# A first attention block copied out in two parts, and three pieces of a fused kernel's schedule moved

## The chip, the core and the metric

One core of a Trainium2 chip. The metric is the device time of one execution in microseconds (us); the median of several runs is compared.

## What is computed

Three stages follow one another: attention over 2 x 768 tokens with 8 heads of 64, in which a query sees the 8 first keys and the 96 before it; then a feed-forward block with a mish gate; then four experts with relu, weighted by probabilities. Everything is fp32.

```python
scores = scale * np.matmul(q, k.transpose(0, 1, 3, 2)) + bias
scores = np.where(keep, scores, -1000000000.0)
a = np.exp(scores - np.max(scores, axis=-1, keepdims=True))
x = np.matmul(a / (np.sum(a, axis=-1, keepdims=True) + 1e-09), v)
...
h = x @ w_in
g = h * np.tanh(np.where(h > 20.0, h, np.log1p(np.exp(np.minimum(h, 20.0)))))
x = g @ w_out
...
p = domain_probs / (domain_probs.sum(-1, keepdims=True) + 1e-09)
for e in range(E):
    out += p[:, e:e + 1] * (np.maximum(x @ w1[e], 0.0) @ w2[e])
```

## The kernel before, in words

The 1536 tokens are three blocks of 512. An attention tile is 128 queries by two heads (a pair); a block has 16 pairs. Weights come in chunks: 16 of the feed-forward block, 32 of the experts. Each chunk is one step: a hidden product (`hidden`, L648: 12 matmuls of 128x512) into a PSUM bank, an activation, and an output product (`project`, L737: 12 matmuls). Fast matmuls take fp32 values as two halves, a high one (names ending in h, a ScalarE cast) and a low one (ending in l, a subtraction). `part` makes them of a weight chunk: ACT casts `wh` (L630), POOL subtracts `wl` in two operations (L633).

The kernel runs in this order. First the attention of block 0 and its feed-forward steps 0 to 15 (`first_block`). Its order is written out by hand as a string, `PLAN`: each letter is one stage of one pair or chunk. `F` copies a row tile of the attention's result from PSUM into `x0` (`take`, L412), four tiles in all, by ScalarE; the last copy is what the first hidden product (L778) waits for. `Q` is the last output product (L825), which ends the block: `end_ffn` copies the result to `y0h` on ACT (L754) and subtracts `y0l` on DVE (L755), in four operations each. Letters near the end of the string begin the second attention, of blocks 1 and 2: `j` splits one more pair's q and k (ACT casts qs and kh, L239 and L241; the subtractions are on POOL for the first two pairs, on DVE from the third), `z` makes the probabilities on DVE, `4` is `norm` and `parts`, `2` and `3` are scores and softmax of the first pair, `6` is the step of a round that multiplies by the values. `norm` takes the reciprocal of the sums on DVE (L192, L193) and scales the probabilities p: on ACT for the first three pairs (L198), on POOL for the others (L200). `parts` splits pairs up to two ahead, and the values v (ACT L254, POOL L255).

Then a loop over the remaining steps s. From s = 16 the expert steps of block 0 run, and each carries one round of the second attention: scores of pair r (L265, L266), softmax (`gather` of an older pair's result on DVE L329 and L332, with casts on ACT L333 and POOL L334; then L279 on DVE and exponentials on ACT, L290), transposes of pair r - 1 on PE (L205) with their cast on ACT (L302) and subtraction on DVE (L303), norm of pair r, parts, and the value product of pair r - 2 (L312), copied by ACT (L320). Three steps (`EXTRA`, s = 27, 35 and 43) carry two rounds, one before the step's own. The weight chunk two steps ahead is parted at the head of every step. PE, ACT, DVE and POOL each take their instructions in the order in which the program issues them. A transpose of pair r reads p after its scaling; POOL stands at whatever instruction is next in its order.

Of the kernel before, what the change touches and what calls it, by code (L numbers as in the profile page):

```python
# [16 lines left out]
P = 128  # L17
B, H, S, D = 2, 8, 768, 64
DM = H * D
NP = H // 2  # L20
NT = S // P
NTOK = B * S
TB = 512
# [20 lines left out]
    "SSYXXESYSEXSEDXNXESNTDCTXSENAZNEXATTSCZEDAXANSFSNEXTTDCNEZAXANTETSCZaADXNAtSFNTEXSCTXEAZSEDAVSVaXTTX"  # L44
    "CSEZAEADVVFTXTCEZAAaDVVTtTCaAZtAFttttttHecttHanltueHvgtcetatntluHvcgnlyettPuvaacHttentPyytlHguvacttH"
    "tbagetnluseyvPcgtbPtbybnPbbbbsluavHcgtnltyyeuvPcgsHnlytaPtuvgtaPyttetatcntstHlseuvcHgtstneluaHvePHcn"
    "tgtluyvcPsgtenlHuvcwgatnliseuvPcHyttjrntlegryyPuyvcsnlwH12yPguevcngl3wuvghPhwwwowowz4Qywj6"
)

AFTER = {  # L50
# [109 lines left out]
class Pair:  # L160
# [47 lines left out]
    def take(self):  # L208

        xh, xl = self.body.x[self.t]  # L210
        at = slice(None), self.pr, slice(self.col, self.col + P)
        heads = [(slice(j * 64, (j + 1) * 64), slice(j * P, (j + 1) * P)) for j in range(2)]
        for r, c in heads:
            self.nc.scalar.copy(xh[at][r, :], self.o[r, c])
        for r, c in heads:
            self.nc.vector.tensor_tensor(xl[at][r, :], self.o[r, c], xh.bitcast(F32)[at][r, :], ALU.subtract)
# [120 lines left out]
class FirstPair(NarrowPair):  # L337
# [71 lines left out]

    def take(self, engine):  # L410

        engine(self.body.x0[:, :, self.col:self.col + P], self.body.o.rearrange("p (n q) -> p n q", n=NP))  # L412


class WidePair(Pair):
# [128 lines left out]
class Body:  # L544
# [420 lines left out]
    def flush(self):  # L965
        for run in self.later:
            run()
        self.later = []
# [35 lines left out]
    def late_block(self, project):  # L1004
# [22 lines left out]
        for run in held[:2]:  # L1027
            run()
# [9 lines left out]
        for run in held[2:]:  # L1038
            run()
# [30 lines left out]
    def first_block(self, ready, now):  # L1070
# [4 lines left out]
        then = Attention(self, self.pair, 1, NB - 1)  # L1075
        n = dict.fromkeys("SXEDNTCAFHecnluvgPatwbsyrhoz", 0)
# [103 lines left out]
        def begin_next(k):  # L1180
# [5 lines left out]
            "S": scores, "X": pair("biased"), "E": pair("exps"), "D": inverse, "N": scale(nc.gpsimd), "V": scale(nc.vector), "T": pair("trans"),  # L1186
            "C": pair("copy", nc.scalar.copy), "Z": pair("copy", nc.vector.tensor_copy), "A": pair("av"),
            "F": take(nc.scalar.copy), "G": take(nc.vector.tensor_copy), "a": begin, "t": convert, "w": part,
            "Y": warm, "H": hidden, "e": self.mish_exp, "c": self.mish_cap, "n": self.mish_n, "l": self.mish_r,
            "u": self.mish_u, "v": self.mish_v, "g": self.gate_first, "P": project, "Q": last,  # L1190
# [1 line left out]
            "b": x_part, "s": split, "y": store,  # L1192
            "z": lambda k: self.probabilities(), "r": second, "h": self.mish_hi, "o": self.mish_lo,
            "1": lambda k: then.ahead(), "2": lambda k: then.scores(), "3": lambda k: then.softmax(),
            "4": lambda k: (then.norm(), then.parts()), "5": lambda k: then.trans(), "6": lambda k: then.av(),
        }
        same = dict(Z="C", G="F", V="N")
        for token in PLAN:
# [11 lines left out]
    def run(self):  # L1210
# [6 lines left out]
        last = len(steps)  # L1217
# [16 lines left out]
        def now(what, upto):  # L1234
            while ready[what] < min(upto, last):
                for _ in getattr(self, what)(ready[what]) or ():
                    pass
                ready[what] += 1
# [3 lines left out]
        if self.first:  # L1242
            att, done = self.first_block(ready, now)
            s0 = NF1
        else:
            att, done, s0 = Attention(self, self.pair, 0), 0, 0
# [4 lines left out]
        for s in range(s0, last):  # L1251
            if s == NF1 and not att:
                att = Attention(self, self.pair, 1, NB - 1)
            if s == need[1]:
                while att and att.round():
                    pass
                att = None
                self.attending.close()
                self.late = self.ctx.enter_context(tc.tile_pool(name="late", bufs=1))
            if self.wide and s < NF1:  # L1260
                while ready["narrow"] < min(s + 3, NF1):
                    now("fetch", ready["narrow"] + 1)
                    now("narrow", ready["narrow"] + 1)
            if ffn_at(s - 1) and done < s:
                self.mish_newton(s - 1)
            if s == NF1 and done < s:

                self.mish_hi(s - 1)
                self.mish_lo(s - 1)
                self.project(s - 2)  # L1270
                self.project(s - 1)
                done = s
            now("part", min(s + 3, last))
            if att:
                att.ahead()
            rest, att = (att, None) if s == need[0] - 2 else (None, att)
            extra = att and s - NF1 in EXTRA
            if extra:
                att.scores()
                att.softmax()  # L1280
            self.hidden(s)
            if extra:
                att.trans()
                att.norm()
                att.parts()
                att.av()
                att.ahead()
            if att:
                att.scores()
            if ffn_at(s):  # L1290
                self.mish_exp(s)
            else:
                self.relu_hi(s)
            if att:
                att.softmax()
            if not ffn_at(s):
                self.relu_lo(s)
            if ffn_at(s - 1) and done < s:
                self.mish_hi(s - 1)
            if ffn_at(s):  # L1300
                self.mish_cap(s)
                self.mish_n(s)
                self.mish_r(s)

                if ffn_at(s - 1):
                    self.mish_lo(s - 1)
            if not self.wide or ready["narrow"] == NF1:
                now("fetch", s + 6)
            follow = bool(s0) and s == NF1 + 1
            if follow:  # L1310
                self.project(done)
                done += 1
            if att and not extra:
                att.trans()
                att.norm()
                att.parts()
            if ffn_at(s - 1) and not ffn_at(s) and done < s:
                self.mish_lo(s - 1)
            if not follow and done <= s - (1 if s0 and att and s < need[0] - 2 else 2):
                self.project(done)  # L1320
                done += 1
            if extra:
                att.trans()
                att.norm()
                att.parts()
            if att and not att.av():
                att = None
            att = att or rest
            for task in {8: (("weights", 0, "in"), ("weights", 1, "in")), 6: (("sums", 0),), 5: (("sums", 1),),
                         3: (("part", 0, "in"), ("weights", 0, "out")), 2: (("part", 0, "sums"),),  # L1330
                         1: (("part", 1, "in"),)}.get(last - s, ()):
                getattr(self, "late_" + task[0])(*task[1:])
# [64 lines left out]
```

## Time and profile before

| what | value |
|---|---|
| median of 3 runs | 882.5 us (881.11 to 882.75) |
| the profiled execution | 882.74 us |
| its span, first to last instruction | 880.9 us |
| mean granted clock of TensorE | 0.997 of full speed |
| busy share of PE, DVE, ACT, POOL | 98%, 65%, 56%, 46% |
| HBM read, written | 97.02 MB, 28.31 MB |

The span is the time between the first and the last instruction; the profiled execution is 1.8 us longer. PE is TensorE's matmuls, PEld its weight loads, ACT ScalarE, DVE VectorE, POOL GpSimd, SP the engine that issues most transfers. In rows of a timeline the bracket is the time for which the engine sat idle before the instruction, and what ended it. Neighbouring records of one engine overlap by up to 0.1 us or so, since an operation begins while the one before it drains.

### The profile page before, as it was taken

How to read it: one execution, taken by the hardware profiler on the slowest of the kernel's cores; microseconds unless marked ns; L12 is line 12 of the kernel's file. 1: busy time of each engine (PE TensorE's matmuls, PEld its weight loads, DVE VectorE, ACT ScalarE, POOL GpSimd, SP SyncE). 2: the span in 40 equal slices, each digit the busy share in tenths (PEclk: the TensorE clock that was granted, in tenths of full speed). 3: DMA queues.
4: the chain of work that ended last, by engine and by line, in shares of the span. 5: the costliest groups of instructions: out<-in, count | busy, mean ns of one | idle time of the engine just before them, and what ended most of it. 6: DMA issues, size and time to landing. Idle time of an engine off the chain costs nothing.

```text
span 880.9 us, 11412 instructions
## 1 busy us (share of the span) xinstructions
PE 865.2 (98%) x3892; PEld 677.8 (77%) x3892; DVE 575.1 (65%) x1108; ACT 495.1 (56%) x971; POOL 407.5 (46%) x431
## 2 busy tenths in 40 slices
PE   8899998999999999999999999999999999999997
PEld 4545656888888888888888888788888888888886
DVE  6999996766777775566656667645555555555555
ACT  6667576878877777577675567533333333333330
POOL 4001333777776877555310225554455555544420
PEclk9999999999999999999999999999999999999999
DMA  8479782444444442888555640511111111111002
GB/s 316 171 247 282 263 310 96 162 171 145 168 144 145 167 168 73 307 290 289 223 194 198 241 167 1 186 54 48 48 48 48 49 57 62 49 48 48 1 1 99
DMA packets 40579, 127.47 MB, mean 145 GB/s; under 512 B 4160, under 2 KB 6976, under 8 KB 38464
## 3 DMA queue, kind: packets, MB, share of 16 engines
q1 hardware_dynamic: 39648, 125.32, 40.6%
q0 software_dynamic: 720, 1.31, 0.8%
q8 instruction: 32, 0.52, 0.2%
q14 instruction: 35, 0.29, 0.1%
q10 hardware_dynamic: 144, 0.02, 0.0%
HBM read 97.02 MB, written 28.31 MB: 142 GB/s over the span
## 4 chain that ended last, share of the span: by engine, by line
PE 80%; DVE 9%; DMA 4%; issue 2%; ACT 2%; POOL 1%; SPq 0%; DVEq 0%; ACTq 0%; POOLq 0%
PE acc_l L985 20%; PE acc L737 19%; PE h L648 18%; PE ha L934 9%; PE hx L934 7%; DMA wfirst<-w 2%; PE pt L205 2%; DVE w L612 2%; PE o L312 1%; DVE w L614 1%; DMA qk<-in_qk 1%; DVE w L610 1%; PE acc L821 1%; DVE nr L688 1%; PE s L266 1%
## 5 line engine op out<-in xcount | busy, mean ns | idle before, releaser
L633 POOL TENSOR_TENSOR wl<-w,wh 128x512 fp32r<-128x512 f32 x94 | 123.6, 1335 | 67.5 <-ACT wh L630 54.3
L838 DVE SCALAR_TENSOR_TENSOR big<-acc_l,prob,big 128x512 f32<-128x512 f32 x120 | 88.8, 746 | 78.9 <-PE acc_l L985 78.7
L917 POOL TENSOR_TENSOR zl<-wout,zh 128x512 fp32r<-128x512 f32 x32 | 40.9, 1303 | 85.2 <-ACT zh L915 85.2
L917 POOL TENSOR_TENSOR sumsl<-bias,sumsh 128x512 fp32r<-128x512 f32 x32 | 42.7, 1355 | 69.3 <-ACT sumsh L915 69.3
L947 ACT COPY raw<-ha 128x512 f32<-128x512 f32 x33 | 19.4, 586 | 79.6 <-PE ha L934 79.6
L684 DVE SCALAR_TENSOR_TENSOR nr<-e,n 128x512 f32<-128x512 f32 x48 | 34.1, 711 | 44.1 <-ACT n L679 43.8
L664 ACT ACTIVATE e<-h 128x512 f32<-128x512 f32 x48 | 28.1, 586 | 60.8 <-PE h L648 25.5
L200 POOL TENSOR_SCALAR p<-p,st 128x256 f32<-128x256 f32 (+1 forms) x58 | 41.5, 726 | 36.6 <-ACT v L254 31.9
L648 PE MATMUL h<-y0h,wh 128*128 128x512 f32 x128 | 51.0, 398 | 2.1 <-ACT y0h L754 1.9
L737 PE MATMUL acc<-wh,gh 128*128 128x512 f32 x128 | 52.4, 409 | 0.0
L648 PE MATMUL h<-y0l,wh 128*128 128x512 f32 x128 | 51.0, 398 | 0.7 <-DVE y0l L755 0.7
L648 PE MATMUL h<-y0h,wl 128*128 128x512 f32 x128 | 50.9, 398 | 0.0
L985 PE MATMUL acc_l<-zh,gh 128*128 128x512 f32 x128 | 50.7, 396 | 0.0
L985 PE MATMUL acc_l<-zh,gl 128*128 128x512 f32 x128 | 50.5, 394 | 0.0
L630 ACT CAST wh<-w 128x1024 fp32r<-128x1024 f32 x48 | 50.1, 1045 | 0.7
L985 PE MATMUL acc_l<-zl,gh 128*128 128x512 f32 x128 | 50.4, 394 | 0.0
L737 PE MATMUL acc<-wh,gl 128*128 128x512 f32 x128 | 50.2, 392 | 0.0
L985 PE MATMUL acc_l<-zh,gl_late 128*128 128x512 f32 (+1 forms) x128 | 50.0, 391 | 0.0
L985 PE MATMUL acc_l<-zh,gh_late 128*128 128x512 f32 (+1 forms) x128 | 50.0, 391 | 0.0
L737 PE MATMUL acc<-wl,gh 128*128 128x512 f32 x128 | 50.0, 390 | 0.0
L737 PE MATMUL acc<-gh,wh 128*128 128x512 f32 x128 | 49.8, 389 | 0.0
L737 PE MATMUL acc<-gh,wl 128*128 128x512 f32 x128 | 49.8, 389 | 0.0
(254 smaller groups left out, 2521.3 us busy)
## 6 DMA issues: line engine op xcount, KB each, us to landing
w<-in_wts SPq DMA_DIRECT2D x32, 512.0 KB, 4.6
raw<-in_qkv SPq DMA_DIRECT2D x32, 512.0 KB, 3.6
big<-in_wff SPq DMA_DIRECT2D x10, 1024.0 KB, 6.4
wfirst<-w SPq DMA_DIRECT2D x16, 512.0 KB, 11.0
w<-wfirst SPq DMA_DIRECT2D x16, 512.0 KB, 4.7
wkeep<-wh SPq DMA_DIRECT2D x16, 512.0 KB, 4.0
wkeep<-wl SPq DMA_DIRECT2D x16, 512.0 KB, 3.0
wh<-wkeep SPq DMA_DIRECT2D x16, 512.0 KB, 3.2
```

The source lines that it names most:

```text
L200: nc.gpsimd.tensor_scalar(p, p, r, 0.0, ALU.mult, ALU.add)
L630: (nc.vector.tensor_copy if copy == "vector" else nc.scalar.copy)(hi, w)
L633: getattr(nc, engine or "gpsimd").tensor_tensor(lo[:, c], w[:, c], hi.bitcast(F32)[:, c], ALU.subtract)
L648: nc.tensor.matmul(ps, a[:, c], r[:, kc, :], start=m == 0, stop=m == 3 * KC - 1)
L664: nc.scalar.activation(e, self.h[s], AF.Exp, scale=0.5)
L684: nc.vector.scalar_tensor_tensor(self.nr[s], e, 1.0, n, ALU.add, ALU.mult)
L737: nc.tensor.matmul(acc[:, h], a, r, start=opens and k == 0 and m == 0, stop=closes and k == len(chunks) - 1 and m == 2)
L838: nc.vector.scalar_tensor_tensor(o, acc, p, o, ALU.mult, ALU.add)
L917: nc.gpsimd.tensor_tensor(lo[:, c], w[:, c], hi.bitcast(F32)[:, c], ALU.subtract)
L934: nc.tensor.matmul(ps, a[:, c], r[:, kc, :], start=opens and n == 0, stop=n == 5, skip_group_check=True)
L947: nc.scalar.copy(t[(1, 6, 7).index(m)], ps)
L985: nc.tensor.matmul(o, a[:, c], r[:, w], start=n == 0, stop=n == 5)
```

## The change

The last of the four copies of the first attention's result is made in two operations, the first of them of one block of 128 columns. In the plan, `j` (one more pair split) goes ahead of `z`, `4` is `norm` alone, and `parts` becomes a letter of its own, `7`, behind `Q`. In the loop, `norm` goes ahead of `trans`, and in the three steps with two rounds the parting of the weight chunk goes from the head of the step to behind the second softmax.

```diff
-    "...tgtluyvcPsgtenlHuvcwgatnliseuvPcHyttjrntlegryyPuyvcsnlwH12yPguevcngl3wuvghPhwwwowowz4Qywj6"
+    "...tgtluyvcPsgtenlHuvcwgatnliseuvPcHyttjrntlegryyPuyvcsnlwH12yPguevcngl3wuvghPhwwwowowjz4Q7yw6"
...
     def take(self, engine):
 
-        engine(self.body.x0[:, :, self.col:self.col + P], self.body.o.rearrange("p (n q) -> p n q", n=NP))
+        o = self.body.o.rearrange("p (n q) -> p n q", n=NP)
+        for n in (slice(0, 1), slice(1, NP)) if self.col + P == TB else (slice(0, NP),):
+            engine(self.body.x0[:, n, self.col:self.col + P], o[:, n, :])
...
-            "4": lambda k: (then.norm(), then.parts()), "5": lambda k: then.trans(), "6": lambda k: then.av(),
+            "4": lambda k: then.norm(), "7": lambda k: then.parts(), "5": lambda k: then.trans(), "6": lambda k: then.av(),
...
-            now("part", min(s + 3, last))
             if att:
                 att.ahead()
             rest, att = (att, None) if s == need[0] - 2 else (None, att)
             extra = att and s - NF1 in EXTRA
-            if extra:
+            if not extra:
+                now("part", min(s + 3, last))
+            else:
                 att.scores()
                 att.softmax()
             self.hidden(s)
             if extra:
+                att.norm()
                 att.trans()
-                att.norm()
                 att.parts()
                 att.av()
                 att.ahead()
...
             if not ffn_at(s):
                 self.relu_lo(s)
+            if extra:
+                now("part", min(s + 3, last))
...
             if att and not extra:
+                att.norm()
                 att.trans()
-                att.norm()
                 att.parts()
...
             if extra:
+                att.norm()
                 att.trans()
-                att.norm()
                 att.parts()
```

The orders of PE and SP are the same before and after. ACT at the end of the first block, before (qs4_1 and kh4_1 are the second pair's operands, qs4_2 and kh4_2 the third's, v4_0 the first pair's values, acc0 the output product's banks):

```order
L630 CAST wh18_1186<-w18_973 128x1024
L198 ACTIVATE p4_0_1159<-p4_0_1159,st4_0_1161 128x256 x2
L239 CAST qs4_1_1201<-raw0_122 128x256
L241 CAST kh4_1_1203<-raw0_122 128x512
L239 CAST qs4_2_1208<-raw1_123 128x256
L241 CAST kh4_2_1210<-raw1_123 128x512
L254 CAST v4_0_1215<-raw0_122 128x2x2x64
L754 CAST y0h_1242<-acc0_0_683 128x512
```

And now, on the same engine at the same place:

```order
L632 CAST wh18_1187<-w18_974 128x1024
L239 CAST qs4_1_1193<-raw0_122 128x256
L241 CAST kh4_1_1195<-raw0_122 128x512
L198 ACTIVATE p4_0_1160<-p4_0_1160,st4_0_1162 128x256 x2
L756 CAST y0h_1233<-acc0_0_684 128x512
L756 CAST y0h_1233<-acc0_1_685 128x512
L756 CAST y0h_1233<-acc0_2_686 128x512
L756 CAST y0h_1233<-acc0_3_687 128x512
L239 CAST qs4_2_1243<-raw1_123 128x256
L241 CAST kh4_2_1245<-raw1_123 128x512
L254 CAST v4_0_1250<-raw0_122 128x2x2x64
```

Two casts went ahead of the scaling, three behind the four y0h copies. On DVE the third pair's subtractions went behind the four y0l subtractions in the same way.

POOL in the first step with two rounds, before (p7_0 and p7_1 are the probabilities of the step's two pairs, wl29 the low half of the weight chunk):

```order
L633 TENSOR_TENSOR wl29_2160<-w29_1948,wh29_2159 128x512 x2
L334 TENSOR_TENSOR x1l_1388<-of6_1_2170,x1h_1387 128x128
L200 TENSOR_SCALAR p7_0_2177<-p7_0_2177,st7_0_2179 128x256 x2
L255 TENSOR_TENSOR v7_0_2214<-raw0_122,v7_0_2214 128x2x128
L334 TENSOR_TENSOR x1l_1388<-of6_2_2230,x1h_1387 128x128
L200 TENSOR_SCALAR p7_1_2237<-p7_1_2237,st7_1_2239 128x256 x2
```

And now, at the same place:

```order
L334 TENSOR_TENSOR x1l_1389<-of6_1_2166,x1h_1388 128x128
L200 TENSOR_SCALAR p7_0_2173<-p7_0_2173,st7_0_2175 128x256 x2
L255 TENSOR_TENSOR v7_0_2210<-raw0_122,v7_0_2210 128x2x128
L334 TENSOR_TENSOR x1l_1389<-of6_2_2226,x1h_1388 128x128
L635 TENSOR_TENSOR wl29_2243<-w29_1949,wh29_2242 128x512 x2
L200 TENSOR_SCALAR p7_1_2233<-p7_1_2233,st7_1_2235 128x256 x2
```

The weight's two subtractions went from ahead of the first pair's scaling to right ahead of the second pair's.

ACT in the same step, now (gh27 is the step's relu, wh29 the cast that the subtractions wait for; before, it stood ahead of the first pair's x1h cast):

```order
L714 ACTIVATE gh27_2224<-h27_2180 128x512
L333 CAST x1h_1388<-of6_2_2226 128x128
L290 ACTIVATE p7_1_2233,st7_1_2235<-t7_1_2234,st7_1_2235 128x256 x2
L632 CAST wh29_2242<-w29_1949 128x1024
L302 CAST pt7_0_2270<-pt7_0_2265 128x4x128
```

The cast now stands behind the second pair's exponentials and ahead of the cast of the first pair's transposes.

## Rows read from the trace of the kernel before

**Rows 1.** Page, part 1: busy us (share of the span) xinstructions of each engine

```profile
PE 865.2 (98%) x3892; PEld 677.8 (77%) x3892; DVE 575.1 (65%) x1108; ACT 495.1 (56%) x971; POOL 407.5 (46%) x431
```

**Rows 2.** Chain of waits: start us, us, what, one product of a step

```profile
171.34 2.76 PE h L648 x12
```

**Rows 3.** PE's waits, 125 to 345 us: releaser, us in total, times, longest

```profile
PE pt L205 <- POOL p L200: 1.1, 3, 0.4
...
PE h L783 <- ACT halfh L790: 0.5, 1, 0.5
```

**Rows 4.** Timeline, 139 to 150 us: start us, us, engine line op out<-in xcount [idle <-releaser]

```profile
139.99 0.17 DVE L193 RECIPROCAL st<-st 128x2 f32<-128x2 f32 x1
...
140.25 0.91 ACT L198 ACTIVATE p<-p,st 128x256 f32<-128x256 f32 x2 [2.00 <-DVE st L193]
...
141.37 0.40 PE L825 MATMUL acc<-gl,zh 128*128 128x512 f32 x1
...
142.83 1.58 DVE L246 TENSOR_TENSOR kl<-raw,kh 128x512 fp32r<-128x512 f32 x1
...
143.01 2.03 ACT L754 CAST y0h<-acc 128x512 fp32r<-128x512 f32 x4
...
143.64 0.50 PE L648 MATMUL h<-y0h,wh 128*128 128x512 f32 x1 [1.87 <-ACT y0h L754]
...
144.34 2.47 DVE L755 TENSOR_TENSOR y0l<-acc,y0h 128x512 fp32r<-128x512 f32 x4
...
145.07 0.50 PE L648 MATMUL h<-y0l,wh 128*128 128x512 f32 x1 [0.70 <-DVE y0l L755]
...
149.05 0.28 PE L265 MATMUL s<-kh,qs 128*128 128x256 f32 x1
```

**Rows 5.** Windows: stretch, then busy us of PE, PEld, DVE, ACT, POOL; granted clock; DMA

```profile
145.50:148.90 3.40, 3.40 (x10) 2.63 (x9) 1.31 (x3) 0.00 (x0) 0.75 (x1) 0.50 0.80 295
```

**Rows 6.** Timeline at 37 us, the first block's last copy

```profile
36.44 1.22 DVE L614 SCALAR_TENSOR_TENSOR w<-big,w 128x1024 int32<-128x1024 int32 x1
37.28 0.58 ACT L412 COPY x<-o 128x512 f32<-128x512 f32 x1 [0.66 <-PE o L407]
...
37.92 8.42 PE L778 MATMUL h<-x,w 128*128 128x512 f32 x19 [0.69 <-ACT x L412]
```

**Rows 7.** Timeline, 218 to 231 us, first extra round

```profile
218.38 0.54 ACT L320 COPY p<-o 64x128 f32<-64x128 f32 x2 [0.62 <-PE o L312]
...
220.08 2.54 POOL L633 TENSOR_TENSOR wl<-w,wh 128x512 fp32r<-128x512 f32 x2 [0.54 <-ACT wh L630]
...
220.29 0.30 ACT L333 CAST x1h<-of 128x128 fp32r<-128x128 f32 x1 [0.29 <-DVE of L332]
...
226.97 0.57 ACT L302 CAST pt<-pt 128x512 fp32r<-128x512 f32 x1
...
228.71 1.51 POOL L200 TENSOR_SCALAR p<-p,st 128x256 f32<-128x256 f32 x2 [2.43 <-ACT v L254]
...
230.27 0.55 PE L205 MATMUL pt<-ident,p 128*128 128x128 f32 x3 [0.41 <-POOL p L200]
```

**Rows 8.** Timeline of PE at 167 us

```profile
167.57 0.55 PE L205 MATMUL pt<-ident,p 128*128 128x128 f32 x3 [0.26 <-POOL p L200]
```

**Rows 9.** Page, part 5: ScalarE's cast of a weight chunk, busy us, mean ns

```profile
L630 ACT CAST wh<-w 128x1024 fp32r<-128x1024 f32 x48 | 50.1, 1045 | 0.7
```

**Rows 10.** Timeline, 284 to 288 us, second extra round

```profile
284.91 0.57 ACT L302 CAST pt<-pt 128x512 fp32r<-128x512 f32 x1
...
286.65 1.51 POOL L200 TENSOR_SCALAR p<-p,st 128x256 f32<-128x256 f32 x2 [2.42 <-ACT v L254]
```

**Rows 11.** Timeline, 341 to 345 us, third extra round

```profile
341.54 0.56 ACT L302 CAST pt<-pt 128x512 fp32r<-128x512 f32 x1
...
343.27 0.93 POOL L200 TENSOR_SCALAR p<-p,st 128x256 f32<-128x256 f32 x2 [2.27 <-DVE st L193]
...
344.37 0.60 PE L205 MATMUL pt<-ident,p 128*128 128x128 f32 x4
```

More of the change, by code (lines that the diff above doesn't have):

```diff
@@ L46 @@
     "tbagetnluseyvPcgtbPtbybnPbbbbsluavHcgtnltyyeuvPcgsHnlytaPtuvgtaPyttetatcntstHlseuvcHgtstneluaHvePHcn"
-    "tgtluyvcPsgtenlHuvcwgatnliseuvPcHyttjrntlegryyPuyvcsnlwH12yPguevcngl3wuvghPhwwwowowz4Qywj6"
+    "tgtluyvcPsgtenlHuvcwgatnliseuvPcHyttjrntlegryyPuyvcsnlwH12yPguevcngl3wuvghPhwwwowowjz4Q7yw6"
 )
```

## The prediction

> **What bounds the kernel now.** I read the page first: PE is busy for 98% of the span, the other engines for 46 to 65% [rows 1]. So a change off PE is worth what it takes from, or adds to, PE's waits and PE's rate, and nothing else. The chain of waits shows the rate where nothing disturbs it: twelve 128x512 matmuls of one step's hidden product in 2.76 us, 0.23 each [rows 2]. The list of PE's waits between 125 and 345 us, the stretch that the change touches, is short [rows 3]. Two of its lines matter here: the transposes wait for POOL's scaled probabilities three times (1.1 us together), and one product of the first block waits 0.5 us for ScalarE. The two waits behind the first block's end are in the timeline: PE's last output matmul is issued at 141.37, and the next product starts at 143.64 after 1.87 us of idling for the first y0h copy, then stops 0.70 us more for the first y0l subtraction [rows 4]. And this pause costs twice: the granted clock of the following stretch is 0.50, which is 1.2 instead of 2.4 GHz, with PE busy throughout [rows 5]. From the third matmul at 145.07 to the scores at 149.05 there are ten matmuls in 3.98 us, 0.40 each; at 0.23 they would take 2.3. A fall of the clock costs 1.7 us here.
>
> **The change, part by part.** PE's and SP's own orders stay as they are; only what ACT, DVE and POOL do, and when, moves.
>
> *The last copy in two.* Before, the copy of 128x512 takes 0.58 us and the first product starts at 37.92, after 0.69 us of waiting for it [rows 6]. A cast of 128x128 on this engine takes 0.30 [rows 7], so that operand would be there some 0.3 us sooner; the other three blocks are due only after the first block's matmuls. But the same matmul also needs the first weight chunk, and DVE's last operation on that one ends at 36.44 + 1.22 = 37.66 [rows 6]. That caps the gain at about 0.2 us. At the far end of this stretch PE waits 0.5 us for a ScalarE copy that does not come from PE [rows 3], so a PE that is 0.2 ahead waits 0.2 longer there. I take 0; the ends are 0 and -0.2, and the extra operation on ACT is covered by ACT's wait for that product.
>
> *The hand-over at 140 us.* Before, five casts of the coming attention stand on ACT between the scaling (from 140.25) and the y0h copies (from 143.01), and on DVE the third pair's difference (142.83, 1.58 us) stands ahead of the y0l subtractions (144.34) [rows 4]. The change moves two of the casts into the 2.00 us in which ACT waits for DVE's reciprocal, and three behind the y0h copies; DVE's difference goes behind the y0l subtractions. The new times: the reciprocal is there at 139.99 + 0.17, the scaling ends at 140.25 + 0.91 = 141.1 (records overlap a little), the first y0h copy follows. In the trace the first product starts 0.63 after that copy's start (143.01 to 143.64), so now at 141.7, when PE has just issued its last output matmul. DVE is free and starts on y0l at 141.7; its first result reached PE 0.73 after its start before (144.34 to 145.07), so 142.45 now, and the fourth one comes 3 x 0.62 later (2.47 for four), at 144.3 [rows 4]. PE has one matmul left then: the scores start at 144.6, against 149.05. That is 4.4 us: 1.9 of idling, 0.8 of the second wait, and 1.7 because a PE that hardly stops keeps its clock. What was moved back is needed later: the third pair's operands are ready on DVE some 2 us behind 144.2 (1.58 for the larger one, as before), and are due at the scores behind the next product, another 2.76 and a few small matmuls later, near 148; the value cast's reader comes later still. I see no wait that takes the place. Bounds: -2.7 if the clock falls all the same, -4.6 if nothing waits at all.
>
> *Norm ahead of the transposes.* The reciprocal's two small DVE operations (0.17 each) [rows 4] go ahead of a subtraction that waits for ACT's cast anyway, so POOL can scale about a microsecond sooner. That removes the 0.26 us at 167.57 [rows 8]. I take -0.3 with the restart; the ends are 0 and -0.5.
>
> *The weight parts in the three extra rounds.* Here the change adds a wait. Before, ACT's cast of the weight chunk stood at the head of the round, in time in which ACT then waited for DVE anyway: the next cast comes 0.29 after it, released by DVE [rows 7]. Taking it away brings the chain of the round forward by nothing, since the chain starts with PE's output (218.38, released by PE) [rows 7]. Now the cast stands behind the second pair's exponentials, and POOL's pair of subtractions for that chunk stands between them and the second pair's scaling, for which PE's transposes already waited in rounds one and two. Round one: ACT is free behind the exponentials at 226.97; the two small operations on DVE now run inside a wait, for which I take 0.2 off; the cast takes 1.05 [rows 9]; POOL's subtractions 2.54; the scaling 0.93 to 1.51. The sum with 0.93 is 231.3, and PE went on at 230.27: +1.0 [rows 7]. Round two: 284.91 - 0.3 + 1.05 + 2.54 + 0.93 = 289.1 against 286.65 + 1.51 = 288.2: +1.0 [rows 7, 10]. Round three had no wait: 341.54 + 1.05 + 2.54 + 0.93 = 346.1 against transposes at 344.37, whose second half is due 0.1 later: +1.6 [rows 11]. Together +3.6. I take 0.93 for the scaling because POOL reaches it later, when DVE is done with its own two-input subtraction; in the third round, where no pair is left to subtract, it takes 0.93 before too [rows 11]. At 1.51 the rounds cost 0.6 more each, +5.3. The other end is nothing at all, rival one.
>
> The Trainium skill (GPSIMD Engine Reference, Specifications) says that GpSimd shares its SBUF interfaces with VectorE and contends with VectorE instructions of two SBUF inputs. The trace agrees as far as it goes (1.51 with such an instruction about, 0.93 without one); by that rule alone, with DVE beside it, the sum would take the +5.3.
>
> **Sum.** The profiled execution took 882.74: -4.4 - 0.3 + 3.6 = -1.1. The median of the runs is 882.5, 0.24 lower; on that scale the forecast is 881.4. What a measurement of this kernel can tell from no change is about 0.2%, 1.8 us. So the likeliest case is a small gain that is not clearly told from none.
>
> **Rivals.**
>
> One: the extra rounds cost nothing. The ACT chain would have to start sooner once the weight cast has left the head of the round, by the full 3.6 of cast and subtractions, or POOL would have to have slack. For it: POOL idled 2.43 us ahead of the scaling at 228.71 [rows 7]. Against: the new work is 2.54 plus 1.05, and it cannot start before the exponentials. The time: 882.5 - 4.7 = 877.8.
>
> Two, the slower one: the clock falls at the three new waits. By the sums above PE would wait 1 to 1.5 us in each round, and 0.4 more between its transposes, not far from the 1.87 and 0.70 behind which the clock fell at the hand-over [rows 4, 5]. Against it: PE is busy up to each wait and right behind it. Each fall costs the 1.7 of above. One gives 883.1, two 884.8, three 881.4 + 5.1 = 886.5; from the second on the kernel is slower than before.
>
> The Trainium skill (TensorE: Matmul & The Clock Gate, Part 1: The HAM clock gate) says that the low clock is the default and that PE's activity is what lifts it. By that rule every pause of PE is a candidate, and all three falls would give 886.5; the hand-over agrees (0.50 behind the pause), while the three short waits of now, up to 0.4 us, show no fall.
>
> Three: the hand-over gains less, because the clock falls in spite of the shorter pause, or POOL's half of the second pair is late for the scores. For it: the reciprocal's wait on DVE stays, and it lies ahead of everything else. The gain would be 2.7, the time 883.1.
>
> That the change does not do what it says I leave out: the order of every engine shows it.
>
> **How the numbers follow.** Forecast 0.55, rival one 0.17, rival two 0.18 (0.07 for one fall, 0.11 for two or three), rival three 0.10. The forecast's own range is 879.6 to 883.1: the lower end with a scaling that waits for less, the upper one with the scaling at 1.51. About 0.21 of its 0.55 lies below 880.7, where a gain would show. Faster: 0.21 + 0.17 = 0.38. Slower: 0.11 and 0.03 from the upper ends = 0.14. The same: 0.48. The range goes down to rival one, 877.8, and up to two falls, 884.8.
>
> **What would show it.** Right: the first product behind the first block starts within 0.2 us of PE's last output matmul, the granted clock stays at 1.00 there, and the scores come some 4.4 us sooner. The wait at 167.57 is gone. In each of the three extra rounds the list of PE's waits has the transposes on POOL's scaling with 1 us or more, and POOL's subtractions of the weight stand right ahead of that scaling. Wrong: a granted clock of 0.50 in one of these rounds, POOL's scaling ending no later than before relative to the round's start, a new wait of PE for y0l, or a first product that starts by 0.2 sooner at 38 us with the gain still there at 125.

## The result and the profile after

The changed kernel takes 887.13 us (median of 4 runs, 886.09 to 887.48) against 881.81 of the kernel before in the same comparison; the ratio is 1.0058 (95% interval 1.0044 to 1.0072). It is slower by 0.6%, outside the forecast's range. The profiled execution took 887.48, 4.74 more than that of before. The page's line of busy times, beside [rows 1]:

```profile
PE 867.5 (98%) x3892; PEld 679.0 (77%) x3892; DVE 590.6 (67%) x1108; ACT 495.1 (56%) x972; POOL 401.0 (45%) x431
```

PE is still the engine that counts. What the shares do not show is that its instructions now come sooner at 150 us and later at 350. The same places in both profiled executions, by PE's timeline:

| PE starts | before | after | difference |
|---|---|---|---|
| scores behind the hand-over | 149.05 | 144.60 | -4.45 |
| hidden product behind the old stall at 167.57 | 171.17 | 166.26 | -4.91 |
| first round with two pairs | 217.89 | 212.98 | -4.91 |
| its output product behind the transposes that wait | 230.58 | 227.48 | -3.10 |
| next hidden product | 233.90 | 232.38 | -1.52 |
| second such round: that output product | 288.52 | 289.44 | +0.92 |
| next hidden product | 291.82 | 294.34 | +2.52 |
| third such round: that output product | 344.72 | 349.18 | +4.46 |
| next hidden product | 348.05 | 352.50 | +4.45 |
| end of the span | 880.9 | 885.7 | +4.8 |

The hand-over and the stall behind it came out as forecast. By the table, from the start of the first round to each next hidden product, the three rounds cost 3.39, 4.04 and 1.93; that is 9.36 where 3.6 was forecast. The hand-over in the timeline after, the answer to [rows 4]:

```profile
140.00 0.91 ACT L198 ACTIVATE p<-p,st 128x256 f32<-128x256 f32 x2 [1.18 <-DVE st L193]
140.82 2.03 ACT L756 CAST y0h<-acc 128x512 fp32r<-128x512 f32 x4
...
141.42 2.48 DVE L757 TENSOR_TENSOR y0l<-acc,y0h 128x512 fp32r<-128x512 f32 x4 [1.51 <-ACT y0h L756]
141.44 0.50 PE L650 MATMUL h<-y0h,wh 128*128 128x512 f32 x1
...
144.60 0.28 PE L265 MATMUL s<-kh,qs 128*128 128x256 f32 x1
```

The copies start right behind the scaling, PE goes on without a bracket, and the scores come at 144.60, where the forecast had put them. Not all of the 4.45 belongs to the hand-over: the last output product ahead of it was issued at 141.37 before and at 141.11 after. From there to the scores it is 7.68 before and 3.49 after, so the hand-over itself gives 4.19. The windows of the same stretch show a PE that never stops and a clock of 1.00 (columns: PE, PEld, DVE, ACT, POOL busy in the window, granted clock, DMA share, GB/s):

```profile
140.00:142.00 2.00, 2.00 (x9) 1.21 (x7) 0.58 (x1) 2.00 (x5) 1.84 (x3) 1.00 0.00 0
142.00:144.00 2.00, 2.00 (x9) 1.52 (x9) 1.97 (x5) 1.98 (x5) 1.14 (x1) 1.00 0.00 0
144.00:146.00 2.00, 2.00 (x15) 1.78 (x14) 1.97 (x5) 0.71 (x2) 1.95 (x2) 1.00 0.12 14
```

The loss, in the first of the three rounds, in the timeline after (beside [rows 7]):

```profile
221.95 1.04 ACT L632 CAST wh<-w 128x1024 fp32r<-128x1024 f32 x1
...
223.06 2.71 POOL L635 TENSOR_TENSOR wl<-w,wh 128x512 fp32r<-128x512 f32 x2 [1.81 <-ACT wh L632]
224.67 1.65 DVE L246 TENSOR_TENSOR kl<-raw,kh 128x512 fp32r<-128x512 f32 x1
225.75 1.37 POOL L200 TENSOR_SCALAR p<-p,st 128x256 f32<-128x256 f32 x2
226.72 1.00 PE L205 MATMUL pt<-ident,p 128*128 128x128 f32 x4 [1.95 <-POOL p L200]
...
228.38 0.63 PE L739 MATMUL acc<-wh,gh 128*128 128x512 f32 x1
...
282.50 0.71 PE L312 MATMUL o<-pt,v 128*128 128x256 f32 x4 [0.65 <-DVE of L332]
...
288.68 1.02 PE L205 MATMUL pt<-ident,p 128*128 128x128 f32 x4 [1.98 <-POOL p L200]
...
345.37 2.53 POOL L635 TENSOR_TENSOR wl<-w,wh 128x512 fp32r<-128x512 f32 x2 [1.80 <-ACT wh L632]
347.88 0.94 POOL L200 TENSOR_SCALAR p<-p,st 128x256 f32<-128x256 f32 x2
...
348.42 1.00 PE L205 MATMUL pt<-ident,p 128*128 128x128 f32 x4 [1.37 <-POOL p L200]
```

Read it downwards: POOL idles 1.81 us for the cast, subtracts for 2.71, only then scales, and PE stands for 1.95. Then the matmuls behind it take 0.63 a record instead of 0.39. The later rows are the second round (at 282.50 and 288.68) and the third. The windows say why the matmuls are slower:

```profile
226.00:228.00 2.00, 1.15 (x6) 0.90 (x7) 1.88 (x8) 1.03 (x3) 2.00 (x4) 1.00 0.00 0
228.00:230.00 2.00, 2.00 (x6) 1.58 (x5) 1.72 (x4) 1.96 (x7) 2.00 (x2) 0.53 0.50 166
230.00:232.00 2.00, 2.00 (x7) 1.54 (x6) 1.90 (x5) 0.74 (x2) 2.00 (x5) 0.62 0.95 328
...
290.00:292.00 2.00, 2.00 (x6) 1.57 (x5) 1.73 (x4) 2.00 (x7) 2.00 (x2) 0.50 0.52 160
...
350.00:352.00 2.00, 2.00 (x10) 1.65 (x9) 0.69 (x1) 0.10 (x1) 2.00 (x3) 1.00 0.33 123
```

Behind the first two waits the clock is at its lower level with PE busy throughout, and the output product takes 4.42 and 4.43 us; behind the third wait, of 1.37, it stays at 1.00 and the product takes 2.85. Two falls cost 1.57 + 1.58 = 3.15 of the 9.36.

### The profile page after: what moved, and what is told of

The parts are those of the page before. It is cut to its first block, busy times and chain, and to the rows that moved or that the text cites. A ratio compares the mean times of both kernels' runs of the same rounds, so it can differ in the third digit from the quotient of the medians.

```text
span 885.7 us, 11439 instructions
## 1 busy us (share of the span) xinstructions
PE 867.5 (98%) x3892; PEld 679.0 (77%) x3892; DVE 590.6 (67%) x1108; ACT 495.1 (56%) x972; POOL 401.0 (45%) x431
## 4 chain that ended last, share of the span: by engine, by line
PE 84%; DVE 5%; DMA 3%; issue 2%; ACT 2%; POOL 2%; SPq 0%; DVEq 0%; POOLq 0%; ACTq 0%
PE acc_l L987 20%; PE acc L739 19%; PE h L650 18%; PE ha L936 9%; PE hx L936 7%; PE h L780 3%; PE acc L823 3%; PE pt L205 2%; PE o L312 1%; DMA wfirst<-w 1%; DMA qk<-in_qk 1%; ACT p L290 1%; PE h L785 1%; PE acc L827 1%; PE s L266 1%
## 5 line engine op out<-in xcount | busy, mean ns | idle before, releaser
L739 PE MATMUL acc<-gl,wh 128*128 128x512 f32 x128 | 49.8, 389 | 0.0
```

Source lines behind the costliest of these rows:

```text
L739: nc.tensor.matmul(acc[:, h], a, r, start=opens and k == 0 and m == 0, stop=closes and k == len(chunks) - 1 and m == 2)
```

## The experiments

### Which part of the change costs, and which gives

The first four kernels take the change apart. In `e1_head` the parting of the chunk goes back to the head of the step, all else stays:

```diff
-            if not extra:
-                now("part", min(s + 3, last))
-            else:
+            now("part", min(s + 3, last))
+            if extra:
                 att.scores()
...
-            if extra:
-                now("part", min(s + 3, last))
```

> The changed kernel with the parting of the weight chunk put back to the head of the three steps with two rounds; the rest of the change stays. Theory A (the late parting is the whole loss: waits of the transposes for POOL's scaling, 1.8 + 2.4 + 1.9 us, and two falls of the clock of 1.6 behind them): the three rounds cost what they cost before, the time is the median of before less 4.9, 876.9 (876.3 to 877.8), the list of PE's waits has the transposes on POOL with 1.1 us in all at most, and the granted clock is 1.00 in all three rounds. Theory B (the norm ahead of the transposes, or the other order on DVE, has its share, as the new wait of a value product for DVE's addition suggests): 879 to 886, and some of the clock falls stay.

Measured: 877.16 us (876.79 to 878.72), ratio to before 0.9952 (0.9938 to 0.9965). Theory A. These are the only waits of PE that are left between 125 and 345 us:

```profile
PE h L785 <- ACT halfh L792: 0.6, 1, 0.6
PE o L312 <- DVE of L332: 0.3, 1, 0.3
PE h L650 <- DVE st L279: 0.2, 1, 0.2
```

No transposes wait for the scaling, and the clock does not fall in the rounds. What the norm's new place brings against itself is the wait of a value product for DVE's addition: 0.3 here, 0.7 in the changed kernel, and 1.0 in two waits in `e4_norm_only` and `e10_no_take` below. This version is faster than both kernels.

`e2_part_only` is the converse, the kernel before with the late parting alone (the same lines put in):

> The kernel before with the late parting of the weight chunk in the three steps with two rounds as its only change. Theory A: the whole loss of the rounds, 9.4 us, or a little more since the norm stands behind the transposes here: 881.8 + 9.4 = 891.2 (890 to 893), with the waits for POOL's scaling at 2 us each and the clock at 0.5 behind at least two of them. Theory B (the loss needs the norm in its new place too): under 888.

Measured: 890.16 (888.28 to 891.46), ratio 1.0089 (1.0075 to 1.0102). Theory A again: the late parting by itself costs 8.9 at the median. In its profile the output products behind the waits take 4.43 and 4.42 in rounds one and two.

`e3_plan_only` has the plan's new letters alone:

```diff
-    "...wwwowowz4Qywj6"
+    "...wwwowowjz4Q7yw6"
...
-            "4": lambda k: (then.norm(), then.parts()), ...
+            "4": lambda k: then.norm(), "7": lambda k: then.parts(), ...
```

> The kernel before with the new letters in the plan as its only change (one more pair split ahead of the probabilities, the parts behind the last output product). Theory A: the whole gain of the hand-over, 1.9 us of idling, 0.8 of the second wait and 1.7 of the clock: 881.8 - 4.4 = 877.4 (876.9 to 877.9), the scores at 144.6 in the profile. Theory B (the cast ahead of the transposes and the copy in two are needed for it): 878.5 to 880.

Measured: 878.75 (878.41 to 879.8), ratio 0.9966 (0.9954 to 0.9978). In the profile the scores start at 144.30 with the clock at 1.00, so the plan alone makes the hand-over, as theory A says. The median gains only 2.5, which theory B's 878.5 to 880 covers; the two levels of the kernel before, further down, explain most of that. What the norm's place adds to it is 1.6 with the copy in two (877.16 against 878.75).

`e4_norm_only` has the norm ahead of the transposes alone, at all three places:

```diff
+                att.norm()
                 att.trans()
-                att.norm()
```

> The kernel before with the norm ahead of the transposes in every round as its only change. Theory A: the stall at 167.57 goes, 0.3 to 0.5 us, and in the rounds with two the scaling comes a little sooner: 881.3 (880.8 to 881.7). Theory B (the norm in its new place holds up the transposes' subtraction on DVE in the rounds with two and a value product waits for it): 882 to 885.

Measured: 880.95 (879.62 to 882.03), ratio 0.9993 (0.9984 to 1.0002): no difference that can be told. The waits for POOL are gone, but two waits of value products for DVE's addition stand in their place:

```profile
PE o L312 <- DVE of L332: 1.0, 2, 0.6
```

Four of its 11 executions (879.62 to 880.5) lie below all 71 of the kernel before that are counted below, so a small gain is likely, but the medians do not show it.

### Is it PE's idling that lets the clock fall?

`e5_fill` gives PE something useless to do while it waits (the lines that set `fill` for the three steps are left out):

```diff
         pt = self.body.bank(f"pt{self.u}", 0)
+        if self.body.fill:
+            for _ in range(8):
+                nc.tensor.matmul(pt, *self.body.fill, start=True, stop=True)
         for c in range(self.nk):
```

> The changed kernel with eight more 128x512 matmuls on PE ahead of the transposes of each of the three steps that wait for POOL's scaling: the step's own first weight slice by the high half of its input, written into the bank that the transposes then overwrite, 24 of them in all, 5.5 us at 0.23 each, and of no use. Theory A (PE's idling ahead of the transposes is what lets the clock fall behind them): they stand in time in which PE idles (1.95, 1.98 and 1.37 us), the output products behind the transposes take 2.85 instead of 4.42 and 4.43 us at a granted clock of 1.00, and the kernel gets faster by 3.1 us less some 0.5 in the third round where the wait is shorter: 887.1 - 2.7 = 884.4 (883.7 to 885). Theory B (the fall has to do with the transposes, the values products or the load of the other engines, not with the idling): the products stay at 4.4 and the time is 887 to 888.

Measured: 884.28 (883.95 to 884.88), 2.85 below the changed kernel though PE does 24 matmuls more. PE's timeline of the first round:

```profile
224.35 2.02 PE L298 MATMUL pt<-y0h,wh 128*128 128x512 f32 x8
226.54 1.00 PE L205 MATMUL pt<-ident,p 128*128 128x128 f32 x4 [0.17 <-POOL p L200]
...
228.54 0.39 PE L742 MATMUL acc<-wh,gl 128*128 128x512 f32 x1
```

The transposes start at the same point of the round, the matmuls behind them take 0.39 again, and the product 2.83 (2.84 in round two). Theory A: with the same transposes and the same work on the other engines, the clock stays up in this profile once PE's idle time is filled. The Trainium skill (TensorE: Matmul & The Clock Gate, Part 1: The HAM clock gate) says that the low clock is the default and that activity releases it; this run agrees, with 2.83 and 2.84 instead of 4.42 and 4.43.

### Why the waits were longer than forecast

The forecast had the scaling at 0.93; it took 1.37 in rounds one and two, and POOL's subtractions 2.71 instead of 2.54, beside a DVE subtraction of k that took 1.65. In the kernel before it took 0.85 at this place:

```profile
229.02 0.85 DVE L246 TENSOR_TENSOR kl<-raw,kh 128x512 fp32r<-128x512 f32 x1
```

`e9_one_input` makes DVE's two subtractions there plain copies:

```diff
+        if self.body.single:
+            engine.tensor_copy(self.qs[64:128, :], self.q[64:128, :])
+            engine.tensor_copy(self.kl, self.kh.bitcast(F32))
+            return
         engine.tensor_tensor(self.qs[64:128, :], self.q[64:128, :], self.qs.bitcast(F32)[64:128, :], ALU.subtract)
...
```

> The changed kernel in which DVE's two subtractions of the pair that is split behind the second scaling of a step with two rounds (the differences of q and of k, two SBUF operands each) are plain copies, of one operand, of the same sizes and at the same place; the low halves of two pairs are therefore not computed. Theory A (POOL's scaling took 1.37 instead of 0.94, and its subtractions 2.71 instead of 2.53, because DVE's two-operand subtraction of k, itself 1.65 instead of 0.85, runs beside them; the third round, which has no such pair, shows 0.94 and 2.53): in rounds one and two the scaling takes 0.94 and the subtractions 2.53, the waits are 0.5 to 0.6 shorter each, 887.1 - 1.1 = 886.0 with both falls of the clock, 883 if the shorter waits let the clock stand. Theory B (they are slow for another reason): 1.37 and 2.71 as before, 887.1.

Measured: 885.57 (883.1 to 886.58). The waits are 1.55 and 1.59 instead of 1.95 and 1.98, about two thirds of what theory A forecast, and behind both the clock still falls in this profile (the products take 4.42 each). The timeline shows why it is not more:

```profile
222.97 2.58 POOL L639 TENSOR_TENSOR wl<-w,wh 128x512 fp32r<-128x512 f32 x2 [1.81 <-ACT wh L636]
224.45 1.38 DVE L247 CAST kl<-kh 128x512 fp32r<-128x512 f32 x1
225.53 1.10 POOL L200 TENSOR_SCALAR p<-p,st 128x256 f32<-128x256 f32 x2
```

POOL's scaling still takes 1.10, and the copy, at 1.38, is slower than the 0.85 of the subtraction in the kernel before: the copy gets in POOL's way too, so this control was not clean. The Trainium skill (VectorE: DVE Perf Modes, Mode 2×_2P) says that an operation of one source between SBUF tensors can use both of VectorE's read ports, so that one operand is no proof of one port; the 1.10 and the 1.38 agree. `e13_zeros` therefore lets DVE read nothing (`engine.memset(..., 0.0)` in the place of both copies):

> As in the run with copies, but at that place DVE writes zeros of the same sizes and reads nothing; the low halves of two pairs are not computed. Theory A (POOL and DVE hold each other up when both read SBUF with more than DVE's first operand): in rounds one and two the scaling takes 0.94 instead of 1.37 and POOL's subtractions 2.53 instead of 2.71, PE's waits are 1.4 instead of 1.95 and 1.98, as in the third round, the clock falls in fewer executions: 884.5 (883 to 886). Theory B (the slower POOL operations have another reason): 1.10 to 1.37 as before, 885.6 to 887.1.

Measured: 883.13 (882.48 to 884.12), 4.0 below the changed kernel. Its first round, and two of its windows:

```profile
222.98 2.54 POOL L639 TENSOR_TENSOR wl<-w,wh 128x512 fp32r<-128x512 f32 x2 [1.81 <-ACT wh L636]
225.49 0.94 POOL L200 TENSOR_SCALAR p<-p,st 128x256 f32<-128x256 f32 x2
```

```profile
226.00:228.00 2.00, 1.84 (x9) 1.47 (x10) 1.76 (x7) 1.85 (x8) 2.00 (x3) 1.00 0.02 4
228.00:230.00 2.00, 2.00 (x12) 1.69 (x11) 1.80 (x5) 1.68 (x5) 2.00 (x3) 1.00 0.84 258
```

The scaling takes 0.94 and the subtractions 2.54, as forecast for an undisturbed POOL; the waits are 1.38 in both rounds, and in this profile the falls are gone: the products take 2.84 and 2.83. So theory A holds, and DVE's two subtractions cost twice, some 0.6 us of wait in each of two rounds, and in the profiles also a fall of the clock behind each. That the length of the wait decides the fall is argued from these profiles (falls behind 1.55 to 1.98 in `e9_one_input` and the changed kernel, none behind 1.37 to 1.39 in the same two and here); the hand-over below shows that one wait can go either way.

### Cast or subtractions, and where else the chunk could go

Three kernels on the changed one. `e7_cast_head` puts only ACT's cast back to the head (the parting is a generator, so its halves can be issued apart):

```diff
             else:
+                halves = begin_part()
                 att.scores()
...
             if extra:
-                now("part", min(s + 3, last))
+                for _ in halves:
+                    pass
```

> The changed kernel with ACT's cast of the weight chunk back at the head of the step and POOL's two subtractions where the change puts them. Theory A (what makes POOL late is that its subtractions wait 1.8 us for the cast): POOL starts them 1.8 us sooner, the scaling is due at or shortly behind the end of the scores, waits of 0.5 us at most, no fall of the clock, 878 (877 to 879). Theory B (2.7 us of subtractions ahead of the scaling cost their length whatever they wait for): waits of 1 us or more in each round, 880 to 884.

Measured: 878.63 (878.39 to 878.96), ratio 0.9958 (0.9944 to 0.9971). Theory A: with the cast done early, most of POOL's 2.5 us of subtractions fits into time in which it idles anyway, and the waits for the scaling are 0.5 each in two rounds. `e6_cast_late` is the other half: the cast late, the subtractions behind the second scaling (`halves = begin_part()` where the change parts, the loop behind the second `att.parts()`):

> The changed kernel with ACT's cast of the weight chunk where the change puts it and POOL's two subtractions behind the second scaling instead of ahead of it. Theory A (the order on POOL is the loss, its scaling stands behind 2.5 to 2.7 us of subtractions that themselves start 1.8 us late): no wait of the transposes for POOL's scaling over 0.3 us, no fall of the clock, 877.2 (876.7 to 878). Theory B (the cast on ACT delays the round's other casts by 1.0 each and DVE behind them, and PE waits for those): 880 to 884.

Measured: 880.4 (880.11 to 881.14), ratio 0.9978 (0.9969 to 0.9988). A miss for theory A, and theory B names the wrong place. The wait of these rounds is gone, but it comes back one round later:

```profile
226.01 5.25 POOL L635 TENSOR_TENSOR wl<-w,wh 128x512 fp32r<-128x512 f32 x4
231.21 0.90 POOL L334 TENSOR_TENSOR x1l<-of,x1h 128x128 fp32r<-128x128 f32 x1
232.10 0.93 POOL L200 TENSOR_SCALAR p<-p,st 128x256 f32<-128x256 f32 x2
...
232.63 1.00 PE L205 MATMUL pt<-ident,p 128*128 128x128 f32 x4 [0.90 <-POOL p L200]
```

Two chunks in a row stand on POOL, and the late cast has pushed the first of them back: POOL idles 1.12 us for ACT's cast of the values, which stands behind it. `e8_behind` moves cast and subtractions behind everything in the round (`now("part", ...)` behind the second `att.parts()`):

> The changed kernel with cast and subtractions both behind the second norm, the transposes and the parts of the three steps. Theory A: nothing of the weight chunk stands ahead of a scaling any more, the waits for POOL go, and with them the falls of the clock: 876.9 (876.3 to 877.7), as with the parting at the head of the step. Theory B (the chunk comes late for the hidden product two steps on, or two chunks in a row on POOL hold up the next scaling): 878 to 882.

Measured: 877.71 (877.5 to 878.13), ratio 0.9948 (0.9935 to 0.9962). Theory A: the four subtractions in a row start 1.2 us earlier in the round than in `e6_cast_late`, and no wait for the scaling is listed. It is as good as the head of the step, and no better.

### The hand-over's clock, and two levels of the kernel before

The 71 executions of the kernel before in these comparisons lie on two levels: 31 between 880.6 and 881.5, 40 between 882.2 and 883.9, none between. The 881.81 of the result is the middle of two executions on each. The run with the norm alone gave a hint. It has the hand-over's waits of 1.88 and 0.70, and yet its windows show the full clock:

```profile
144.00:146.00 2.00, 1.30 (x6) 1.03 (x6) 2.00 (x5) 0.77 (x2) 1.98 (x2) 1.00 0.11 12
146.00:148.00 2.00, 2.00 (x14) 1.77 (x14) 0.68 (x2) 0.60 (x1) 0.00 (x0) 1.00 0.90 352
```

Before, it was 0.50 [rows 5]. The kernel before, unchanged, was profiled three times more:

> The kernel before, unchanged, one look. Its executions lie on two levels 1.5 us apart, 880.7 to 881.4 and 882.3 to 882.8. Theory A (the fall of the clock at the hand-over behind the first block comes in some executions only, as the run with the norm alone suggests, where the same two waits of 1.88 and 0.70 us leave it at 1.00): at about 881 the granted clock from 145 to 148 is 1.00 and the scores start near 147.4, at about 882.6 it is 0.50 and they start at 149.05. Theory B (the levels come from another place): the scores start at 149.05 at either level.

> The kernel before, unchanged, a second look, for the other level. Theory A: the clock from 145 to 148 and the start of the scores tell the level, 147.4 at about 881 and 149.05 at about 882.6. Theory B: the scores start at 149.05 at either level.

> The kernel before, unchanged, a third look. Theory A: at about 881 the granted clock from 144 to 148 is 1.00 and the scores start some 1.5 us sooner behind the first product than at 882.6, where it is 0.50. Theory B: it is 0.50 there at either level.

They took 882.21, 882.31 and 882.88, all three the upper level, and all three have the clock at 0.50 or 0.51 somewhere from 144 to 148. The lower level was not caught in a profile of this kernel. `e14_fill_hand` tests it another way, with matmuls of no use ahead of the first product:

```diff
         self.h[s] = ps = self.bank(f"h{s}")
+        if s == NF1:
+            for _ in range(8):
+                nc.tensor.matmul(ps, wh[:, 0:P], wl[:, 0:512], start=True, stop=True)
         m = 0
```

> The kernel before with eight more 128x512 matmuls, of no use, ahead of the first product behind the first block, in the 1.87 us in which PE idles there. Theory A (the two levels of the kernel before, 880.7 to 881.4 and 882.3 to 882.8, are the fall of the clock at this wait, which comes in some executions): with PE busy the clock stays at 1.00 from 144 to 148 and all executions lie at the lower level, 881.0 (880.5 to 881.6). Theory B (the levels come from elsewhere): both levels stay, or the time rises by the matmuls' 1.84.

Measured: 881.1 (880.8 to 881.51), all 11 executions on the lower level, and in the profile

```profile
144.00:146.00 2.00, 1.28 (x5) 0.73 (x5) 2.00 (x4) 1.17 (x3) 2.00 (x3) 1.00 0.00 0
146.00:148.00 2.00, 2.00 (x11) 1.67 (x11) 0.96 (x2) 0.15 (x1) 0.42 (x1) 1.00 0.84 293
```

Theory A: the upper level is the fall of the clock behind the hand-over's wait, and the same wait brings it in some executions only. From the last output product to the scores it is 7.18 to 7.70 in the four profiles of the kernel before, all with the fall, 6.08 in `e4_norm_only` without it, and 3.49 in the changed kernel. So the hand-over is worth 3.7 to 4.2 against an execution with the fall and 2.6 against one without; `e3_plan_only` was compared with 16 executions, 10 of them without.

### The copy in two

`e10_no_take` is `e1_head` with the last copy in one operation again:

```diff
-        for n in (slice(0, 1), slice(1, NP)) if self.col + P == TB else (slice(0, NP),):
+        for n in (slice(0, NP),):
```

> The changed kernel with the parting of the chunk at the head of every step, as in the first experiment, and the last copy of the first attention's result in one operation again. Theory A (the copy in two is worth nothing, since the first product then waits for the first weight chunk): 877.2, within 0.3 of the first experiment's 877.16, the wait of the first product on the copy instead of on the chunk. Theory B (0.2 are kept): 877.4 to 877.6.

Measured: 877.5 (877.26 to 878.31), ratio 0.9957 (0.9943 to 0.997), against 877.16: too near to tell 0 from 0.3. The waits of the first 345 us say where it goes, here without the split:

```profile
PE o L312 <- DVE of L332: 1.0, 2, 0.6
PE h L780 <- ACT x L414: 0.7, 1, 0.7
...
PE h L785 <- ACT halfh L792: 0.4, 1, 0.4
```

and with it (`e1_head`):

```profile
PE h L785 <- ACT halfh L792: 0.6, 1, 0.6
PE h L780 <- DVE w L616: 0.6, 1, 0.6
...
PE o L312 <- DVE of L332: 0.3, 1, 0.3
```

0.1 is won at the first product, which then waits for the weight chunk, and 0.2 is given back at the later wait. At the last output product of the first block the two profiles are 0.03 apart (141.12 and 141.09). They part by 0.7 only near 279 us, where this one has a wait of 0.64 for DVE's addition; the changed kernel, with the split, has one of 0.65 at the same place, so the copy is not what brings it.

## Why the prediction was wrong, point by point

**Right: the hand-over**, -4.19 from the last output product to the scores where -4.4 was worked out (with 0.8 for the second wait, which is 0.70 in [rows 4]), with the first product at 141.44 and the scores at 144.60. The other 0.26 of the -4.45 was there ahead of it. What the forecast did not know is that 1.6 of it (7.68 against 6.08) is the price of a fall that the kernel before does not have in every execution.

**Right as far as it can be told: the copy in two**, taken at 0, for the reason given: the weight chunk caps it, and the later wait for ScalarE takes it back. One sign that the forecast had named as wrong did appear: the first product starts 0.40 sooner in the profile after (37.52 against 37.92), and 0.26 is still there at 125 us (125.49 against 125.75). But kernels without the split have that later product anywhere from 125.20 (`e3_plan_only`) to 125.87 (`e14_fill_hand`), so this is a difference between executions.

**Right at the stall, more elsewhere: the norm ahead of the transposes.** In the profile the stall at 167.57 is gone (-0.46, where -0.3 was taken and the ends were 0 and -0.5). Where the parting stays at the head of the step, the norm's place with the copy in two brought 1.6 at the median (`e1_head` against `e3_plan_only`): it also takes POOL's 0.4 us waits out of rounds one and two, and the hidden product behind each comes 0.62 sooner. The forecast had no such term, since in its rounds the late parting puts a new wait there.

**Wrong: the weight parts in the three extra rounds, +3.6.** This is the step that failed: the term measured 9.36. The mechanism is the one that was described, the cast behind the exponentials and the subtractions ahead of the scaling; `e1_head` and `e2_part_only` show that the loss goes and comes with the late parting. The term was mis-sized in three places:

- *The clock.* The sum left it at 1.00, because PE is busy up to each wait and right behind it, and made its fall rival two, with 0.11 for two or three of them. It fell twice, for 3.15 us; a clock of 0.50 in a round was one of the forecast's own signs of being wrong. Two falls were priced at 3.4, so that rival's price was near; it was added to waits that were too short, which is why its 884.8 is not 887.
- *The scaling, taken at 0.93.* The reason given was that DVE would be done with its own subtraction by the time POOL gets there. It was not: POOL's subtractions had held DVE up in their turn (1.65 instead of 0.85). With 1.37 for 0.93 and 2.71 for 2.54 this is 0.6 us in each of rounds one and two; the upper end had it, at 1.51, but for all three rounds, where the third, with no pair left to subtract, took 0.94. In the profile of `e13_zeros`, without those 0.6 us, the waits are 1.38 and the clock stands, so they seem to decide the two falls as well. With DVE's reads gone, what is left of the loss at the medians is 883.13 - 877.16 = 6.0.
- *The rest*, 9.36 - 3.6 - 3.15 - 1.2 = 1.4: 0.5 is the value product of round two that now waits 0.65 for DVE's addition, a wait that the forecast did not name (the hidden product behind it starts at 283.22 against 284.22, 1.00 sooner where it had been 1.52), and 0.3 the third round (1.93 for 1.6). The remaining 0.6 is not taken apart.

Against each other the terms left -1.1 in the forecast and +4.74 in the trace. Rival one (nothing lost in the rounds) would have given 877.8; that is near what the kernel does when the parting stays at the head of the step (877.16).

## What to carry to other kernels

Where a step is moved, count what stands behind it on every queue and ask what the other engine will be doing at that very moment: an operation's duration taken from a quiet place is not its duration beside a neighbour that it contends with. A wait of an otherwise busy TensorE is to be priced twice, with and without a fall of its clock, and the sum made for both: a term that makes a wait 0.6 us longer can bring a fall of 1.6 with it. And when a change is several edits, each deserves its own run: here one of four cost 10 us and hid that the other three together gain 4.1.

## What was not expected of the hardware

The same two waits at the hand-over, 1.87 or 1.88 and 0.70 us, were followed by a granted clock of 0.50 in the profile of the kernel before and of 1.00 in that of `e4_norm_only`, whose change lies in the loop behind it. The executions of the kernel before lie on two levels 1.5 us apart, and filling the wait leaves only the lower one. That one kernel does both is worked out from this; no profile of its lower level was taken.

VectorE and GpSimd hold each other up in both directions (DVE's 1.65 and POOL's 1.37 above), and the one that comes first seems to go on unslowed. In `e6_cast_late`:

```profile
224.75 0.69 DVE L246 TENSOR_TENSOR kl<-raw,kh 128x512 fp32r<-128x512 f32 x1
...
224.76 1.29 POOL L255 TENSOR_TENSOR v<-raw,v 128x256 fp32r<-128x256 f32 x1 [1.12 <-ACT v L254]
```

DVE's subtraction takes 0.69, where in the changed kernel, behind POOL, it took 1.65, while POOL's, 0.73 at the same place in `e13_zeros`, takes 1.29, longer by 0.56, most of the 0.69. The Trainium skill (Trainium Architecture — The Big Picture, What this means for kernel authors) calls the port pair that the two share an exclusive lock, not a split of the bandwidth; these two rows agree.

And useless work can pay: 24 matmuls, some 5.5 us of PE's time at 0.23 each, made the changed kernel 2.85 us faster.
